# Gate and up products of ten feature tiles in the last two token blocks: seven half-width products in place of eight over four of five channel chunks, with sums of weights and tokens on VectorE

## The chip, the cores and the metric

The kernel runs on one core of a Trainium2 chip. The metric is the time of one execution on the device in microseconds (us), as the median of several runs. The core has five engines that run side by side and wait for each other by semaphores: PE (TensorE, matrix products into PSUM), DVE (VectorE), ACT (ScalarE), POOL (GpSimd) and SP (which only issues DMAs here). PEld is the loading of weights into PE.

## What is computed

A layer with linear attention and a gated two-layer network without a nonlinearity, on 2048 tokens of 640 channels in bf16:

```python
def _B_ref(x, w_gate, w_up, w_down):
    g = jnp.einsum("bsd,df->bsf", x, w_gate)
    u = jnp.einsum("bsd,df->bsf", x, w_up)
    h = g * u
    return jnp.einsum("bsf,fd->bsd", h, w_down)

x = A_x
h = x + _A_ref(_layernorm(x, axis=-1), A_wqkv, A_w_phi, A_wo)
h2 = h + _B_ref(_layernorm(h, axis=-1), B_w_gate, B_w_up, B_w_down)
return h2
```

`_A_ref` is the attention: query, key and value projections, softmax features of query and key with either sign, a product of key features with values, and its application to the query features. The change touches `g` and `u` of `_B_ref` alone. There are 640 channels (five chunks of 128) and 1536 features (twelve tiles of 128).

## The kernel before

The 2048 tokens are 16 tiles of 128 and four blocks of 512. Keys and values of all tiles come first, then block by block: queries (`q`, `Q`), the attention output (`n`, in `num`), its projection and the second layernorm (`h`, in `watt`), the gate and up products (`f`, in `fu`) and the down product (`d`, `D`). A transposed block of normalized tokens lies in `hT` (channels on the partitions, two buffers), the product of gate and up in `hhT` (features on the partitions, two buffers).

`fu(b, ft, j, n)` makes one feature tile of one block. PE runs two groups of five products (one per channel chunk), gate into the first bank of a PSUM buffer and up into the second. ScalarE copies the gate half to `gate`, and VectorE multiplies it with the up half in PSUM and writes `hhT`. Blocks 1 to 3 take 512 tokens at once, block 0 takes 256 twice.

The down product of most token tiles already uses a scheme of seven block products in place of eight (`down_pair`, with `weight_sums` on GpSimd and `block_sums` on VectorE, named `T` and `S` in the order). There, PE writes a product into a bank, a helper copies the intermediate value out (`snap`), and PE goes on adding to the same bank; VectorE adds copy and bank at the end (`fin`).

All operations are recorded with the data that they read and write, and then placed. What each engine does in which sequence is written out by hand in the table `ORDER`, one list of unit names per engine: `f3.2.0` is feature tile 2 of block 3, and each occurrence of a name stands for the next operation of that unit on that engine. `place` walks the lists, hands out buffers from pools in that sequence (four PSUM buffers of two banks, `p_ps`; two `gate` buffers) and `finish` turns the recorded dependences into semaphore waits. An engine works through its list strictly in sequence, so an instruction that waits holds all that stand behind it on that engine.

Lines: every group of products is issued by the helper `mms` (L620). The copy of the gate is L1093, the gate times up product L1095, the down scheme's copies L1190, its add on GpSimd L1192, its final sums L1197, its differences of `hhT` L1131. `ACT phik L896` are exponentials early in the kernel.

A profile names a tile by the storage it lies in. `BK` is called `phik`: it first holds the key features and later `hhT`, `hT` and the first half of `oT`. `phiqT` holds the transposed query features, `xT` the transposed input (and later the sums of `block_sums` and some of `weight_sums`), `Wp` the projection weights (and later sums of `weight_sums`), `vaug` the values and later the down weights.

Of the kernel before, what the change touches and what calls it, by code (L numbers as in the profile page):

```python
# [62 lines left out]

SNAP = {(3, 0): "AAAV", (3, 1): "AAAV"}
# [19 lines left out]
    "DVE":  # L84
# [323 lines left out]
def _build(ctx, nc, A_x, A_wqkv, A_w_phi, A_wo, B_w_gate, B_w_up, B_w_down, out):  # L408
# [74 lines left out]
    o1 = KH * HALF  # L483
    SH = [[xTf[:, o1 + KH * P * (2 * k + i):o1 + KH * P * (2 * k + i + 1)].rearrange("p (f n) -> p f n", f=KH) for i in range(2)]
          for k in range(4)]

    PS = [ctx.enter_context(nc.psum_tensor("ps%d" % i, [P, 2, 512], FP32)) for i in range(4)]

    p_ps, p_eq, p_ob, p_outb, p_t32, p_gate, p_junk = Pool(4), Pool(3), Pool(2), Pool(2), Pool(2), Pool(2), Pool(1)
# [849 lines left out]
```

## Time and profile before

| what | value |
|---|---|
| median of 3 runs | 274.58 us (273.94 to 274.63) |
| the profiled execution, its own time | 274.22 us |
| its span, first to last instruction | 272.2 us |
| instructions in the span | 5588 |
| PE busy | 266.9 us |
| DVE busy | 195.1 us |
| ACT busy | 139.7 us |
| POOL busy | 127.9 us |
| mean granted PE clock | 1.000 |

The time of a run is the span and what lies around it, 2.0 us in the profiled execution. A row of the timeline gives start, length, engine, line, operation, output and inputs by storage name, shapes, and in brackets how long the engine had been idle before and for whom it waited. A row of the groups gives the count, the busy time, the mean duration in ns, and the idle time before. The duration of a matmul includes its way through the array, in which the next one already runs: what it costs the engine is the distance between two starts.

### The profile page before, as it was taken

The page shows a single profiled execution, that of the slowest core. Times are in us where ns is not written, and L with a number is a line of the kernel's source. Part 1 is how long each engine was busy: PE and PEld are TensorE (multiplying, and loading weights), DVE is VectorE, ACT ScalarE, POOL GpSimd, SP SyncE. Part 2 cuts the span into 40 slices and gives each one's busy share as a digit, 9 for nine tenths or more (in the row PEclk, how much of TensorE's full clock was granted, in tenths as well). Part 3 has the DMA queues.
Part 4 walks back from the last instruction along what each step waited for, and adds up shares of the span by engine and source line. Part 5 has one row for each costly group of instructions (what it writes and reads, how often), then busy time and mean ns, then how long its engine had stood idle before and what let it go on. Part 6 is the DMA issues. An engine that isn't in the chain of part 4 may idle for free.

```text
span 272.2 us, 5588 instructions
## 1 busy us (share of the span) xinstructions
PE 266.9 (98%) x2216; PEld 181.7 (67%) x2229; DVE 195.1 (72%) x383; ACT 139.7 (51%) x261; POOL 127.9 (47%) x177
## 2 busy tenths in 40 slices
PE   8999999999999999999999999999999999999995
PEld 8877687777878887777865555555555464555673
DVE  1899999999999997887886685833754283522673
ACT  2568999999856767548165232164221230411411
POOL 5626989999842349064392833015340220130442
PEclk9999999999999999999999999999999999999999
DMA  7987899904175997445854454300043001001012
GB/s 192 291 148 182 139 281 400 333 2 88 25 106 101 162 287 105 97 80 102 113 116 80 79 104 72 72 2 0 0 96 99 0 0 51 0 6 42 4 69 75
DMA packets 67385, 28.60 MB, mean 105 GB/s; under 512 B 57632, under 2 KB 66080, under 8 KB 67360
## 3 DMA queue, kind: packets, MB, share of 16 engines
q1 hardware_dynamic: 66432, 27.90, 45.5%
q10 hardware_dynamic: 928, 0.35, 0.5%
q8 instruction: 17, 0.28, 0.5%
q14 instruction: 8, 0.07, 0.1%
HBM read 11.82 MB, written 2.62 MB: 53 GB/s over the span
## 4 chain that ended last, share of the span: by engine, by line
PE 78%; DVE 6%; ACT 4%; DMA 3%; POOL 3%; SPq 3%; issue 2%; ACTq 0%
PE ps L620 78%; SPq L516 3%; DMA Wp<-in_A_wqkv_dram 2%; DVE ps L888 1%; ACT phik L896 1%; DMA phiqT<-eq 1%; ACT eq L896 1%; DVE Wp L856 1%; DVE phik L1095 1%; POOL phik L913 1%; ACT vaug L919 1%; ACT junk L613 1%; DVE Sq L950 1%; DVE Ssum L910 1%; POOL eq L962 0%
## 5 line engine op out<-in xcount | busy, mean ns | idle before, releaser
L620 PE MATMUL ps<-phik,Wgu 128*128 128x512 bf16 (+1 forms) x587 | 108.4, 335 | 0.6
L620 PE MATMUL ps<-Wp,xT 128*128 128x320 bf16 (+1 forms) x606 | 88.9, 299 | 0.2 <-ACT phik L896 0.2
L620 PEld LDWEIGHTS ps<-phik,Wgu 128*128 128x128 bf16 x600 | 57.9, 98 | 41.7 <-DVE phik L1095 0.4
L620 PEld LDWEIGHTS ps<-Wp,xT 128*128 128x128 bf16 x606 | 58.3, 98 | 23.8 <-ACT phik L896 0.6
L1095 DVE TENSOR_TENSOR phik<-ps,gate 128x512 bf16<-128x512 f32 (+1 forms) x60 | 34.0, 575 | 40.8 <-PE ps L620 27.8
L1093 ACT ACTIVATE gate<-ps 128x512 bf16<-128x512 f32 (+1 forms) x60 | 29.8, 510 | 61.8 <-PE ps L620 53.6
L1192 POOL TENSOR_TENSOR eq<-eq,x_all 128x320 f32<-128x320 f32 x20 | 15.8, 797 | 65.8 <-ACT eq L1190 65.7
L913 POOL TENSOR_TENSOR phik<-phik,Rk 128x1280 bf16<-128x1280 bf16 x16 | 37.4, 2356 | 6.7 <-DVE Rk L912 6.5
L888 DVE TENSOR_REDUCE ps<-ps 128x1 f32<-128x640 f32 (+1 forms) x32 | 26.2, 821 | 0.9 <-PE ps L620 0.9
L620 PE MATMUL ps<-vaug,phik 128*128 128x63 bf16 (+1 forms) x308 | 26.0, 238 | 0.0
L950 DVE TENSOR_REDUCE Sq<-eq 128x66 f32<-128x1320 bf16 x16 | 24.2, 1509 | 2.5 <-ACT eq L896 2.5
L910 DVE TENSOR_REDUCE Ssum<-phik 128x64 f32<-128x1280 bf16 x16 | 23.5, 1469 | 0.4 <-ACT phik L896 0.2
L620 PEld LDWEIGHTS ps<-vaug,phik 128*128 128x128 bf16 x308 | 18.4, 97 | 6.2
L962 POOL TENSOR_TENSOR eq<-eq,rq 128x660 bf16<-128x660 bf16 x16 | 20.9, 1305 | 0.9
L896 ACT ACTIVATE eq<-ps,nb,rs 128x300 bf16<-128x300 f32 (+2 forms) x26 | 17.4, 692 | 7.1 <-DVE hb L1078 3.5
L1190 ACT ACTIVATE eq<-ps 128x320 f32<-128x320 f32 x20 | 8.5, 437 | 21.7 <-PE ps L620 21.7
L957 POOL TENSOR_TENSOR rq<-Sq,rq 128x33 f32<-128x33 f32 x16 | 4.1, 257 | 32.2 <-DVE rq L956 26.7
L896 ACT ACTIVATE eq<-ps,nb,nrs 128x300 bf16<-128x300 f32 (+2 forms) x26 | 17.4, 698 | 0.0
L613 ACT ACTIVATE junk<-x_all,nmh 128x640 bf16<-128x640 bf16 x14 | 11.6, 825 | 8.7 <-DVE x_all L1069 8.7
L896 ACT ACTIVATE phik<-ps,nb,rs 128x640 bf16<-128x640 f32 x16 | 14.3, 892 | 2.3 <-POOL rs L677 2.0
L896 ACT ACTIVATE phik<-ps,nb,nrs 128x640 bf16<-128x640 f32 x16 | 14.3, 897 | 0.0
L1197 DVE TENSOR_TENSOR outb<-ps,eq 128x320 bf16<-128x320 f32 x22 | 10.3, 485 | 5.6 <-PE ps L620 4.6
(107 smaller groups left out, 311.3 us busy)
## 6 DMA issues: line engine op xcount, KB each, us to landing
x_all<-in_A_x_dram SPq DMA_DIRECT2D x4, 640.0 KB, 10.6
out_dram<-outb SPq DMA_DIRECT2D x14, 160.0 KB, 1.8
Wgu<-in_B_w_gate_dram SPq DMA_DIRECT2D x1, 1920.0 KB, 10.7
Wgu<-in_B_w_up_dram SPq DMA_DIRECT2D x1, 1920.0 KB, 15.9
vaug<-in_B_w_down_dram SPq DMA_DIRECT2D x1, 1920.0 KB, 9.6
Wp<-in_A_wqkv_dram SPq DMA_DIRECT2D x1, 800.0 KB, 5.1
phiqT<-in_A_wqkv_dram SPq DMA_DIRECT2D x1, 800.0 KB, 6.7
Wo<-in_A_wo_dram SPq DMA_DIRECT2D x1, 800.0 KB, 6.4
```

The source lines that it names most:

```text
L613: g.op("ACT", lambda e: e.activation(out=junk[:, v.i, :], in_=in_, func=func, accum_out=acc, **more), rd=rd, wr=wr, use=[v], t=0.73, lat=0.97)
L620: ins = e.matmul(o_, lhsT=l_, rhs=r_, start=s_, stop=p_, skip_group_check=True)
L888: g.op("DVE", lambda e: e.tensor_reduce(out=mx(), in_=src(), axis=AX.XY if len(src().shape) == 3 else AX.X, op=ALU.max, apply_absolute_val ...
L896: g.op("ACT", lambda e, s=s, sc=sc, to=to, of=of: e.activation(out=to(s), in_=of(), func=ACT.Exp, bias=nb[:, i:i + 1], scale=sc[:, t:t + 1 ...
L910: g.op("DVE", lambda e: e.tensor_reduce(out=Ssum[:, vs.i, :], in_=x, axis=AX.X, op=ALU.add), rd=R_phik[t], wr=vs.R, use=[vs], t=1.39, lat=1.5)
L913: g.op("POOL", lambda e: e.tensor_tensor(out=x, in0=x, in1=Rk[:, vr.i, :].unsqueeze(2).to_broadcast([P, 2 * H, DH]), op=ALU.mult), rd=vr.R ...
L950: g.op("DVE", lambda e: e.tensor_reduce(out=Sq[:, vs.i, :].rearrange("p (w g) -> p w g", w=NQ), in_=feat(0, NQ).rearrange("p w (g f) -> p ...
L962: return e.tensor_tensor(out=x, in0=x, in1=rq[:, vr.i, :].rearrange("p (w h) -> p w h", h=HW).unsqueeze(3).to_broadcast([P, NQ, HW, DH]), ...
L1093: g.op("ACT", lambda e: e.activation(out=gate[:, vg.i, 0:P * n], in_=PS[v.i][:, 0, 0:P * n], func=ACT.Copy), rd=[v.R[0]], wr=vg.R, use=[v, ...
L1095: g.op("DVE", lambda e: e.tensor_tensor(out=hhT[:, hb, ft, sl], in0=PS[v.i][:, 1, 0:P * n], in1=gate[:, vg.i, 0:P * n], op=ALU.mult), rd=[ ...
L1192: g.op("POOL", lambda e: e.tensor_tensor(out=slot(x), in0=slot(x), in1=x_all[:, t, c], op=ALU.add), rd=x.R + [R_h[t]], wr=x.R, use=[x], t= ...
L1197: g.op("DVE", lambda e: e.tensor_tensor(out=outb[:, o_.i, HALF * half:HALF * (half + 1)], in0=PS[v.i][:, bk, 0:HALF], in1=slot(y), op=ALU. ...
```

## The change

For ten of the twelve feature tiles (0 to 9) of blocks 2 and 3, `fu` hands over to `fu_seven`. Take gate and up as two rows of weights, chunks 0, 1 and chunks 2, 3 as two columns, and the first and second 256 tokens of the block as two columns of tokens. The plain way has eight products of (two chunks) x (256 tokens); the new one has seven, with four sums of weights and four of tokens:

- weights, made once by `gate_sums` (`G`): G0 = up01 + up23, G1 = gate01 - up01, G2 = G0 - gate01, G3 = gate23 - G2, each for three groups of tiles (0 to 4, 5 to 7, 8 and 9), which lie in three storages that are no longer in use (`phiqT`, `xT`, `Wp`): twelve operations on VectorE;
- tokens, made once for each block by `token_sums` (`H`): H0 = t01' - t01, H1 = t23' - t01', H2 = t23' - H0, H3 = t23 - H2, where the prime means the second 256 tokens: four operations on VectorE.

The fifth chunk stays as it was, one product of 512 tokens for gate and one for up. So a tile has 14 products of 256 columns and 2 of 512, in place of 10 of 512. PE's work on a tile is six operations: gate01 x t01 into the up bank, G0 x H0 into the gate bank, G2 x H2 added to the up bank, gate23 x t23 and G3 x t23' and the fifth chunk in the gate bank, G1 x H1 added to the up bank, up23 x H3 and the fifth chunk in the up bank. Between them ScalarE copies four intermediate halves (256 columns of fp32) to `halves`, in the storage of the second `phiqT` buffer; there are five such copy buffers of 512 columns. PE may add to a bank only after the copy is out. At the end VectorE adds copy and bank for gate (L1196) and for up (L1198), and multiplies the two, bf16 from SBUF (L1200).

The diff, with the table of the order cut to a line:

```diff
+SEVEN = {2: range(10), 3: range(10)}
+WSP = ()
...
-        "f2.11.0 D1.0 f2.6.0 D1.1 f2.7.0 D1.1 f2.6.0 f2.7.0 f3.2.0 f3.2.0 f2.5.0 f2.5.0 D1.1 D1.1 D1.1 D1.1 f3.9.0 D1.1 f3.6.0 "
+        "f2.5.0 f3.2.0 f3.2.0 f3.9.0 f3.9.0 D1.1 f3.9.0 f3.2.0 f3.9.0 f3.2.0 f3.2.0 f3.9.0 f3.6.0 f3.6.0 f3.2.0 f3.0.0 f3.0.0 "
...
+    GW = [(0, 5, [pq[:, 1280 * k:1280 * (k + 1)] for k in range(4)]), (5, 3, [xTf[:, o1 + 768 * k:o1 + 768 * (k + 1)] for k in range(4)]),
+          (8, 2, [Wp[:, k, 0:512] for k in range(4)])]
+    HS = [oTa[:, k, :].rearrange("p (c n) -> p c n", c=2) for k in range(4)]
+    halves = pq[:, NQ * 512:NQ * 512 + 5 * 1024].bitcast(FP32).rearrange("p (i n) -> p i n", i=5)
...
+    p_hb, p_slot, p_half = Pool(2), Pool(8), Pool(5)
...
+        if ft in SEVEN.get(b, ()):
+            return fu_seven(b, ft)
...
+    def gate_sums():
+        for k, (x, y, op) in enumerate((((1, 0), (1, 2), ALU.add), ((0, 0), (1, 0), ALU.subtract), (0, (0, 0), ALU.subtract),
+                                        ((0, 2), 2, ALU.subtract))):
+            for r, (f0, nf, _) in enumerate(GW):
+                U("G%d.%d" % (r, k))
...
+                g.op(eng, lambda e, part=part, x=x, y=y, op=op, r=r, k=k: e.tensor_tensor(out=gw(r, k), in0=part(x), in1=part(y), op=op),
+                     rd=rd, wr=[R_GW[r][k]], t=t, lat=t + 0.12, port=True)
+
+    def token_sums(b):
...
+            g.op("DVE", lambda e, part=part, x=x, y=y, op=op, k=k: e.tensor_tensor(out=HS[k], in0=part(x), in1=part(y), op=op),
+                 rd=rd, wr=[R_HS[k]], t=0.34, lat=0.46, port=True)
+
+    def fu_seven(b, ft):
...
+        v, vg = Buf(p_ps, 2), Buf(p_gate)
+        s = [Buf(p_half, 2) for _ in range(2)]
...
+        def snap(bk, i, h):
+            g.op("ACT", lambda e: e.activation(out=halves[:, s[i].i, 256 * h:256 * (h + 1)], in_=PS[v.i][:, bk, 256:512], func=ACT.Copy),
+                 rd=[v.R[bk]], wr=[s[i].R[h]], use=[v, s[i]], after=HALF_USERS, t=0.3, lat=0.42)
+
+        U("f%d.%d.0" % (b, ft))
+        mm([(raw(0, 0), tok(0, 0), 256, 256)], 1, True)
+        snap(1, 0, 0)
+        mm([(summed(0), toks(0), 256, 256)], 0, True)
+        snap(0, 1, 1)
+        mm([(summed(2), toks(2), 256, 256)], 1)
+        snap(1, 0, 1)
+        mm([(raw(0, 2), tok(2, 0), 0, 256), (summed(3), tok(2, 1), 256, 256), (raw(0, 4), tok(4, 0, 2), 0, 512)], 0)
+        mm([(summed(1), toks(1), 256, 256)], 1)
+        snap(1, 1, 0)
+        mm([(raw(1, 2), toks(3), 0, 256), (raw(1, 4), tok(4, 0, 2), 0, 512)], 1)
+        R_out = R_hhT[hb_][ft]
+        g.op("DVE", lambda e: e.tensor_tensor(out=gate[:, vg.i, :], in0=PS[v.i][:, 0, :], in1=halves[:, s[0].i, :], op=ALU.add),
+             rd=[v.R[0]] + s[0].R, wr=vg.R, use=[v, s[0], vg], t=0.61, lat=0.73)
+        g.op("DVE", lambda e: e.tensor_tensor(out=hhT[:, hb_, ft, :], in0=PS[v.i][:, 1, :], in1=halves[:, s[1].i, :], op=ALU.add),
+             rd=[v.R[1]] + s[1].R, wr=R_out, use=[v, s[1]], t=0.61, lat=0.73)
+        g.op("DVE", lambda e: e.tensor_tensor(out=hhT[:, hb_, ft, :], in0=hhT[:, hb_, ft, :], in1=gate[:, vg.i, :], op=ALU.mult),
+             rd=R_out + vg.R, wr=R_out, use=[vg], t=0.34, lat=0.46, port=True)
...
     weight_sums()
...
+    gate_sums()
     ffn(0)
...
+    token_sums(2)
     ffn(2)
...
+    token_sums(3)
     ffn(3)
```

The table of the order is new for all engines. Two places in block 3 show what it does around the new tiles. The first is on PE, where tiles 0 and 6 of block 3 are made. Before, with `ps` and its number the PSUM buffer, `phik` the tokens and `Wgu` the weights of gate or up, and tile 6 in ps2, tile 0 in ps1, tile 9 in ps3:

```order
L620 MATMUL ps2<-phik,Wgu 128x512 [waits s_DVE]
L620 MATMUL ps2<-phik,Wgu 128x512 x4
L620 MATMUL ps1<-phik,Wgu 128x512 [waits s_DVE]
L620 MATMUL ps1<-phik,Wgu 128x512 x4
L620 MATMUL ps2<-phik,Wgu 128x512 x5
L620 MATMUL ps3<-phik,Wgu 128x512 x5
```

The same place now; `phiqT`, `xT` and `Wp` hold the sums of weights, and tile 0 is in ps2, tile 3 in ps3, tile 6 in ps0:

```order
L1174 MATMUL ps2<-phik,Wgu 128x256 [waits s_ACT]
L1174 MATMUL ps2<-phik,Wgu 128x256
L1174 MATMUL ps2<-phik,phiqT 128x256 x2
L1174 MATMUL ps2<-phik,Wgu 128x512
L1174 MATMUL ps0<-phik,xT 128x256 [waits s_ACT]
L1174 MATMUL ps0<-phik,xT 128x256
L1174 MATMUL ps2<-phik,phiqT 128x256 x2
L1174 MATMUL ps3<-phik,Wgu 128x256 x2
L1174 MATMUL ps3<-phik,phiqT 128x256 x2
L1174 MATMUL ps0<-phik,Wgu 128x256 [waits s_ACT]
L1174 MATMUL ps0<-phik,Wgu 128x256
L1174 MATMUL ps0<-phik,Wgu 128x512
```

Where PE ran five products of one tile in a row and waited for VectorE to free a buffer, it now goes back and forth between three tiles, and waits for ScalarE's copies in the middle of a tile. Between the product in ps0 that is copied (the two with `xT`) and the next one that waits in ps0 stand six products of 256 columns.

The second place is on VectorE, with the tiles of the middle of block 3. Before, each tile has one row (L1095), with a difference for the down product (L1131) and final sums (L1197) between them:

```order
L1095 TENSOR_TENSOR phik<-ps0,gate 128x512 [waits s_ACT,s_PE]
L1095 TENSOR_TENSOR phik<-ps2,gate 128x512 [waits s_ACT]
L1095 TENSOR_TENSOR phik<-ps3,gate 128x512 [waits s_PE]
L1131 TENSOR_TENSOR xT<-phik,xT 128x768
L1095 TENSOR_TENSOR phik<-ps1,gate 128x512 [waits s_ACT]
L1197 TENSOR_TENSOR outb<-ps0,eq 128x320 [waits d_out2,s_POOL,s_PE]
```

Now each tile has three rows, the gate sum (L1196), the up sum (L1198) and their product (L1200); the `phiqT` in a sum is the copy buffer:

```order
L1198 TENSOR_TENSOR phik<-ps1,phiqT 128x512 [waits s_PE]
L1198 TENSOR_TENSOR phik<-ps0,phiqT 128x512 [waits s_PE]
L1200 TENSOR_TENSOR phik<-phik,gate 128x512 [waits s_DVE]
L1196 TENSOR_TENSOR gate<-ps2,phiqT 128x512 [waits s_DVE]
L1200 TENSOR_TENSOR phik<-phik,gate 128x512
L1198 TENSOR_TENSOR phik<-ps2,phiqT 128x512 [waits s_PE]
L1196 TENSOR_TENSOR gate<-ps3,phiqT 128x512 [waits s_DVE,s_ACT,s_PE]
L1198 TENSOR_TENSOR phik<-ps3,phiqT 128x512 [waits s_PE]
L1200 TENSOR_TENSOR phik<-phik,gate 128x512 [waits s_DVE]
L1196 TENSOR_TENSOR gate<-ps1,phiqT 128x512 [waits s_DVE,s_ACT,s_PE]
```

The rows of several tiles are interleaved, and the product of a tile stands one or more rows behind its up sum. An up sum is what frees a PSUM buffer and its copy buffers for the next tile.

More of the change, by code (lines that the diff above doesn't have):

```diff
@@ L1096, in fu, with gw, part @@
              rd=[v.R[1]] + vg.R, wr=R_hhT[hb][ft][j:j + n], use=[v, vg], t=0.073 + 0.134 * n, lat=0.19 + 0.134 * n)
+    def gw(r, k):
+        return GW[r][2][k].rearrange("p (c n) -> p c n", c=2)
+    def gate_sums():
[3 more added lines that the diff above has]
+                U("G%d.%d" % (r, k))
+                def part(q, r=r, f0=f0, nf=nf):
+                    return gw(r, q) if isinstance(q, int) else Wgu[:, q[0], q[1]:q[1] + 2, P * f0:P * (f0 + nf)]
+                rd = R_Wgu + [R_GW[r][q] for q in (x, y) if isinstance(q, int)]
+                eng, t = ("POOL", 0.1 + 0.47 * nf) if r in WSP else ("DVE", 0.06 + 0.14 * nf)
+                g.op(eng, lambda e, part=part, x=x, y=y, op=op, r=r, k=k: e.tensor_tensor(out=gw(r, k), in0=part(x), in1=part(y), op=op),
+                     rd=rd, wr=[R_GW[r][k]], t=t, lat=t + 0.12, port=True)
@@ new lines, in token_sums, with part @@
+    def token_sums(b):
+        hb_ = b % 2
+        for k, (x, y, op) in enumerate((((0, 1), (0, 0), ALU.subtract), ((2, 1), (0, 1), ALU.subtract), ((2, 1), 0, ALU.subtract),
+                                        ((2, 0), 2, ALU.subtract))):
+            U("H%d.%d" % (b, k))
+            def part(q):
+                return HS[q] if isinstance(q, int) else hT[:, hb_, q[0]:q[0] + 2, 256 * q[1]:256 * (q[1] + 1)]
+            rd = [R_HS[q] for q in (x, y) if isinstance(q, int)] + [R_hT[hb_][2 * q[1] + i] for q in (x, y) if not isinstance(q, int)
+                                                                    for i in range(2)]
+            g.op("DVE", lambda e, part=part, x=x, y=y, op=op, k=k: e.tensor_tensor(out=HS[k], in0=part(x), in1=part(y), op=op),
+                 rd=rd, wr=[R_HS[k]], t=0.34, lat=0.46, port=True)
@@ new lines, in fu_seven, with raw, summed, tok @@
+    def fu_seven(b, ft):
+        hb_ = b % 2
+        v, vg = Buf(p_ps, 2), Buf(p_gate)
+        s = [Buf(p_half, 2) for _ in range(2)]
+        r = max(r for r in range(len(GW)) if GW[r][0] <= ft)
+        f0 = P * (ft - GW[r][0])
+        def raw(gu, c0):
+            return lambda c: Wgu[:, gu, c0 + c, P * ft:P * (ft + 1)], R_Wgu[gu]
+        def summed(k):
+            return lambda c: gw(r, k)[:, c, f0:f0 + P], R_GW[r][k]
+        def tok(c0, i, n=1):
+            return lambda c: hT[:, hb_, c0 + c, 256 * i:256 * (i + n)], R_hT[hb_][2 * i:2 * (i + n)]
+        def toks(k):
+            return lambda c: HS[k][:, c, :], [R_HS[k]]
+        def mm(lst, bk, first=False):
+            def f(e):
+                ins, fr = None, first
+                for l_, r_, lo, n in lst:
+                    for c in range(2 if n == 256 else 1):
+                        ins = e.matmul(PS[v.i][:, bk, lo:lo + n], lhsT=l_[0](c), rhs=r_[0](c), start=fr, stop=False, skip_group_check=True)
+                        fr = False
+                return ins
+            t = sum(0.2185 if n == 256 else 0.216 for _, _, _, n in lst)
+            g.op("PE", f, rd=[x for l_, r_, _, _ in lst for x in [l_[1]] + r_[1]], wr=[v.R[bk]], use=[v], t=t, lat=t + 0.15)
+        def snap(bk, i, h):
[19 more added lines that the diff above has]
+             rd=R_out + vg.R, wr=R_out, use=[vg], t=0.34, lat=0.46, port=True)
@@ L1297, in _build @@
     g.alias([r for x in R_S for r in x], R_xT[2:12])
+    g.alias(R_GW[0], [r for x in R_phiqT[0] for r in x])
+    g.alias(R_GW[1], R_xT[11:])
+    g.alias(R_GW[2], R_Wp[0])
+    gate_sums()
     ffn(0)
@@ L1302, in _build @@
     down(0)
+    g.alias(R_HS, R_oT[0])
+    HALF_USERS += [o for x in R_phiqT[1] for r in x for o in r.w + r.r]
+    token_sums(2)
     ffn(2)
```

5 lines of the change are left out of this document (3 added, 2 removed), and 99 rows, old and new, of the table ORDER.

## The prediction

> **What bounds the kernel now.** I read the page first (busy shares, slices, the chain that ended last), then TensorE's waits, then the busy times by stage, then single stretches of the timeline. The page:
>
> ```profile
> PE 266.9 (98%) x2216; PEld 181.7 (67%) x2229; DVE 195.1 (72%) x383; ACT 139.7 (51%) x261; POOL 127.9 (47%) x177
> ...
> DVE  1899999999999997887886685833754283522673
> ...
> PEclk9999999999999999999999999999999999999999
> ...
> PE 78%; DVE 6%; ACT 4%; DMA 3%; POOL 3%; SPq 3%; issue 2%; ACTq 0%
> ```
>
> PE is busy for 98% of the 272.2 us span, at the full granted clock in every slice, and 78% of the chain is PE. VectorE is full only up to about the middle and has gaps behind it. All that PE ever waited for, by the list of waits:
>
> ```profile
> PE ps L620 <- PEq L1324: 0.8, 1, 0.8
> PE ps L620 <- DVE Phi L1003: 0.3, 1, 0.3
> PE ps L620 <- ACT phik L896: 0.2, 1, 0.2
> ```
>
> That is 1.3 us in three waits, none of them in a gate/up product. So the time is the length of PE's queue, and a shorter queue ends sooner unless PE begins to wait. The stages that the change touches (columns: length; busy us and instructions of PE, PEld, DVE, ACT, POOL; clock; DMA share; GB/s):
>
> ```profile
> 139.00:157.00 18.00, 17.89 (x129) 9.95 (x129) 12.54 (x23) 7.46 (x14) 11.86 (x15) 1.00 0.41 84
> 157.00:175.00 18.00, 17.84 (x113) 9.62 (x114) 12.20 (x26) 5.68 (x11) 3.94 (x7) 1.00 0.49 92
> 175.00:198.00 23.00, 22.89 (x135) 13.19 (x135) 12.66 (x24) 9.54 (x21) 7.43 (x13) 1.00 0.00 1
> 198.00:227.00 29.00, 28.79 (x156) 15.55 (x159) 13.16 (x26) 7.13 (x14) 5.44 (x8) 1.00 0.22 57
> 227.00:256.00 29.00, 28.89 (x160) 15.75 (x161) 11.36 (x20) 7.78 (x16) 5.53 (x7) 1.00 0.04 13
> ```
>
> Nearly all gate/up tiles of blocks 2 and 3 lie in the last two rows: PE 57.7 of 58 us, VectorE 24.5, ScalarE 14.9. There is idle time on both helpers to spend there; the question is whether it lies where the new work falls.
>
> **The change, part by part.** *Products removed.* What a matmul costs PE is the distance to the next start, not its own duration. Ten 512-column products (one tile) and ten 256-column ones (a tile of block 0), each with the row behind it:
>
> ```profile
> 132.73 1.25 PE L620 MATMUL ps<-phik,Wgu 128*128 128x256 bf16 x10
> 133.82 1.53 PE L620 MATMUL ps<-Wp,xT 128*128 128x300 bf16 x10
> ...
> 199.25 2.32 PE L620 MATMUL ps<-phik,Wgu 128*128 128x512 bf16 x10
> 201.41 0.98 PE L620 MATMUL ps<-Wp,xT 128*128 128x320 bf16 x6
> ...
> L620 PEld LDWEIGHTS ps<-phik,Wgu 128*128 128x128 bf16 x600 | 57.9, 98 | 41.7 <-DVE phik L1095 0.4 <-issue 0.3
> ```
>
> 201.41 - 199.25 = 2.16 us, 0.216 each; 133.82 - 132.73 = 1.09 us, 0.109 each, with one weight load of 98 ns per product hidden in it. A tile goes from 10 x 0.216 = 2.16 us to 14 x 0.109 + 2 x 0.216 = 1.958 us: 0.202 us saved, 20 x 0.202 = 4.04 us in all. The Trainium skill ("TensorE: Matmul & The Clock Gate", section "Back-to-back issue gap") speaks against it: a stream of load and matmul pairs is said to run at about 81 ns for 128 columns and 131 ns for 512. A straight line gives about 98 ns at 256 (an estimate from that page), a tile would go from 1.31 to 1.63 us, and the change would cost PE 6.4 us. The trace does not agree: 0.216 and 0.109 us in this very loop.
>
> *Copies added on ScalarE, sums on VectorE.* Their nearest rows, by shape, then pairs that ran back to back:
>
> ```profile
> L1095 DVE TENSOR_TENSOR phik<-ps,gate 128x512 bf16<-128x512 f32 x36 | 24.4, 686 | 36.7 <-PE ps L620 23.7 <-ACT gate L1093 13.0
> L1093 ACT ACTIVATE gate<-ps 128x512 bf16<-128x512 f32 x36 | 20.9, 594 | 43.4 <-PE ps L620 35.3 <-DVE phik L1095 8.1
> L1093 ACT ACTIVATE gate<-ps 128x256 bf16<-128x256 f32 x24 | 9.0, 385 | 18.4 <-PE ps L620 18.3
> L1131 DVE TENSOR_TENSOR xT<-phik 128x768 bf16<-128x768 bf16 x14 | 7.8, 569 | 5.8 <-PE ps L620 5.7
> ...
> 133.48 0.66 ACT L1093 ACTIVATE gate<-ps 128x256 bf16<-128x256 f32 x2 [2.96 <-PE ps L620]
> 194.85 1.08 ACT L1093 ACTIVATE gate<-ps 128x512 bf16<-128x512 f32 x2 [1.72 <-PE ps L620]
> ...
> 134.66 0.74 DVE L1095 TENSOR_TENSOR phik<-ps,gate 128x256 bf16<-128x256 f32 x2
> 207.56 1.29 DVE L1095 TENSOR_TENSOR phik<-ps,gate 128x512 bf16<-128x512 f32 x2 [2.20 <-PE ps L620]
> 230.88 1.02 DVE L1131 TENSOR_TENSOR xT<-phik 128x768 bf16<-128x768 bf16 x2
> ```
>
> Subtracting one duration from a pair gives what an instruction costs its queue. ScalarE: 256 columns 0.66 - 0.385 = 0.275, 512 columns 1.08 - 0.594 = 0.49. A tile goes from 0.49 to 4 x 0.275 = 1.10 us; 20 tiles add 12.2 us, to some 27 of about 54 us in the last two stages: room enough. VectorE: a sum from PSUM 1.29 - 0.686 = 0.605 (256 columns: 0.33, so about 0.06 fixed); a bf16 sum of 768 from SBUF 1.02 - 0.55 = 0.47. No 512 one is shown: between 512/768 of it, 0.31, and 0.47; with the fixed 0.06 it is 0.335, which I take. A tile goes from 0.605 to 2 x 0.605 + 0.335 = 1.545 us; 20 tiles add 18.8 us. The eight token sums (512 long) are 8 x 0.335 = 2.7 us. The twelve weight sums (1280, 768, 512 long) are 4 x (0.74 + 0.47 + 0.335) = 6.2 us by the same line; if 1280 ran at the per-element cost of the PSUM rows it would be 4 x 1.4 for that group, 2.6 us more. Most of them fall between 139 and 198 us, where VectorE is busy 37.4 of 59 us; about 45 with them. I cost them at nothing: PE's tiles of blocks 0 and 1 hide them. Were that cover gone, a late weight sum would hold PE by its own length, 0.3 to 0.8 us. The last two stages rise to 24.5 + 18.8 + about 3 = 46 of 54 us.
>
> *The new waits of PE.* Four times per tile PE may add to a bank, or use it again, only after ScalarE has copied it; everything behind it in PE's queue waits along. The paired down products do this already:
>
> ```profile
> 235.46 0.98 PE L620 MATMUL ps<-vaug,phik 128*128 128x320 bf16 x6
> 236.28 1.79 PE L620 MATMUL ps<-Wp,xT 128*128 128x320 bf16 x12
> 236.48 0.44 ACT L1190 ACTIVATE eq<-ps 128x320 f32<-128x320 f32 x1 [1.21 <-PE ps L620]
> 237.29 0.44 ACT L1190 ACTIVATE eq<-ps 128x320 f32<-128x320 f32 x1 [0.38 <-PE ps L620]
> ...
> 31.97 0.91 ACT L896 ACTIVATE phik<-ps,nb,nrs 128x640 bf16<-128x640 f32 x1
> ...
> 32.93 0.85 PE L620 MATMUL ps<-Wp,xT 128*128 128x320 bf16 x5 [0.22 <-ACT phik L896]
> ```
>
> The copy starts 236.48 - 236.28 = 0.20 us after its group's last product has given way; a 256 copy takes 0.385; and PE starts about 0.05 us after ScalarE ends (32.93 - 32.88). A round trip is 0.635 us. In the new order I count the PE work between a copied product and the one that waits for it (0.218 us per pair, 0.652 and 0.434 for the groups with the fifth chunk, 0.815 per down group): of 80 such distances the shortest is 0.654 (three places, one in the piece shown above), the next 0.81. So PE just fits. Each of the three may still expose part of a 98 ns weight load: 0 to 0.3 us, I take 0.2.
>
> *VectorE in block 3.* The tightest stretch, counted in the order from the gate sum of tile 9 to the up sum of tile 5: PE has 29 x 0.218 + 8 x 0.652 + 8 x 0.434 = 15.0 us there, VectorE 15 sums, 8 products and 5 differences before the last sum: 15 x 0.605 + 8 x 0.335 + 5 x 0.47 = 14.1 us. That is 94%: VectorE fits if it never waits, and PE waits for it for a free bank pair or copy buffer if it falls behind by more than these hold. The lower bound of the loss is 0; the upper one takes full durations instead of queue costs (15 x 0.686 + 8 x 0.42 + 5 x 0.569 = 16.5 us; 0.42 is 0.335 plus the 0.08 that a row's duration exceeds its cost by): 1.5 us. I take 0.4, near the lower end, since neighbours in VectorE's new order mostly belong to different tiles. GpSimd's adds can stretch an SBUF difference; that is small and rare:
>
> ```profile
> 221.60 0.79 POOL L1192 TENSOR_TENSOR eq<-eq,x_all 128x320 f32<-128x320 f32 x1 [0.84 <-ACT eq L1190]
> ...
> 222.14 0.66 DVE L1131 TENSOR_TENSOR xT<-phik 128x768 bf16<-128x768 bf16 x1
> 222.84 0.56 DVE L1131 TENSOR_TENSOR xT<-xT,phik 128x768 bf16<-128x768 bf16 x1
> ```
>
> *The re-dealt order.* Elsewhere the same products come in another sequence, with SP's and POOL's steps among them. PE had 1.3 us of waits to win or lose: 0, with 0.3 us to either side.
>
> *Sum.* -4.04 + 0.2 + 0.4 = -3.4 us. The profiled execution took 274.22 us, span 272.2 and 2.0 around it, and would take 270.8. It lies 0.4 us under the median of the runs, 274.58; on that the sum gives 271.2 us.
>
> **The rivals.** *VectorE becomes the limit.* For it: 94% in block 3, and PE holding at most four bank pairs. Against it: plain and down tiles before and behind let VectorE catch up. Price: 1.5 us in block 3 instead of 0.4, up to as much again in block 2; 274.58 - 4.04 + 1.5 = 272.0 to 273.5 us.
>
> *Waits expose weight loads: slower.* In the new order 57 groups of these tiles carry a wait for ScalarE. If a load can't be fetched past such a wait, each shows its 98 ns: 57 x 0.098 = 5.6 us, so 276.1 us. It decides from 4.04 / 0.098 = 41 exposed loads on. Against it: the third of the down groups in the rows above waits for ScalarE, yet the two groups from 236.28 on run through without a gap; there the copy was back 0.18 us early, here 0.02 to 0.2 at the tight places.
>
> *The sums come late.* If weight and token sums push back what VectorE does for block 2's attention output between 139 and 198 us, PE stands until its tokens are there. It takes some 3.4 us of such waits to be at 274.6; with 21 us of idle VectorE in those rows this needs bad placement: 274.0 to 274.9 us.
>
> *The clock drops.* Many short groups with small gaps could lower the granted clock; each us at half clock loses 0.5 us, so 8 us of that take all the gain, 275 us or more. The rows show 1.00 in every stage, also where PE waited. The Trainium skill (the same page, section "A second HAM failure mode: psum-queue depth-cycling") describes such swings; by that rule this kernel is a candidate, but the trace shows no sign so far.
>
> That the products are not really fewer can be left out: the order shows fourteen 256-column and two 512-column products per tile.
>
> **How the numbers follow.** Forecast (270.2 to 272.0) 0.60; VectorE the limit (272.0 to 273.5) 0.24; late sums 0.08; exposed loads 0.06; clock 0.02. The low end is all of 4.04 with 0.3 from the new order: 270.2. The range 270.2 to 273.5 holds 0.84. A measurement of this kernel can tell about 0.3%, 0.8 us, from no change: faster by more than that 0.84, within it 0.08, slower 0.08.
>
> **What would show it.** Right: 160 fewer 512-column and 280 more 256-column gate/up products, these 0.109 us apart; PE busy near 263 us; 80 copies of about 0.385 us; VectorE near 228 us busy (195.1 + 20 x 1.11 for the tiles + some 10 for the sums, by durations); PE's waits under 2 us. VectorE as the limit shows as PE waiting for VectorE in block 3; exposed loads as some 0.1 us before most groups that wait for ScalarE; late sums as a hole before the first tiles of block 2. The prediction is wrong if copies or sums take over 0.1 us more than these rows, or if the 256-column products, now with sums as weights, are further apart.

## The result and the profile after

The changed kernel takes 271.25 us (median of 4 runs, 271.03 to 271.54), the kernel before 274.55 us beside it (273.94 to 274.63). The ratio is 0.9885, with a 95% interval from 0.9868 to 0.9902. Forecast were 271.2 us and faster. The profiled execution took 271.18 us with a span of 269.1: 3.1 us less span than before.

The page of the changed kernel, in the lines that were shown of before:

```profile
PE 264.0 (98%) x2349; PEld 192.5 (72%) x2349; DVE 222.8 (83%) x443; ACT 154.7 (57%) x321; POOL 129.0 (48%) x177
...
DVE  1999999999999897789888669898876678977763
...
PEclk9999999999999999999999999999999999999999
...
PE 83%; DVE 5%; DMA 4%; ACT 3%; POOL 2%; issue 2%; SPq 1%; ACTq 0%; DVEq 0%
```

PE is still the bound (98%, and 83% of the chain), VectorE's valley in the second half of the slices is filled, and the clock stays at full speed. The list of waits has three rows of PE:

```profile
PE ps L641 <- PEq L1437: 0.8, 1, 0.8
PE ps L641 <- DMA vaug<-ob: 0.7, 1, 0.7
PE ps L641 <- DVE Phi L1024: 0.3, 1, 0.3
```

The first and the last stood in the list of before. The wait for a DMA is new, and it is not at a gate/up product. The two stages of the new tiles, and 15 us in the middle of block 3 (columns as in the prediction):

```profile
198.00:227.00 29.00, 29.00 (x222) 21.12 (x220) 20.82 (x43) 15.07 (x45) 7.82 (x12) 1.00 0.13 36
...
223.00:238.00 15.00, 15.00 (x122) 11.40 (x120) 14.14 (x28) 9.27 (x29) 0.21 (x1) 1.00 0.01 2
```

VectorE works 14.14 of 15.00 us there, and PE works all 15. (A product of 256 columns counts as busy for 273 ns and gives way after 109, so a stop of up to 0.16 us does not show in PE's column, and a longer one is 0.16 us longer than a row's brackets say.) The groups of the new work by shape:

```profile
L1181 ACT ACTIVATE phiqT<-ps 128x256 f32<-128x256 f32 x80 | 26.8, 385 | 26.6 <-PE ps L1174 24.0 <-DVE phik L1198 1.3 <-DVE gate L1196 1.1
L1174 PE MATMUL ps<-phik,Wgu 128*128 128x256 bf16 x120 | 22.6, 273 | 0.0
L1196 DVE TENSOR_TENSOR gate<-ps,phiqT 128x512 bf16<-128x512 f32 x20 | 13.7, 686 | 1.1 <-PE ps L1174 0.3 <-ACT phiqT L1181 0.3
L1198 DVE TENSOR_TENSOR phik<-ps,phiqT 128x512 bf16<-128x512 f32 x20 | 13.7, 686 | 3.7 <-PE ps L1174 3.6
L1200 DVE TENSOR_TENSOR phik<-phik,gate 128x512 bf16<-128x512 bf16 x20 | 8.4, 425 | 0.1
...
L1134 DVE TENSOR_TENSOR phiqT<-Wgu 128x1280 bf16<-128x1280 bf16 x2 | 1.6, 790 | 0.0
```

The durations are those taken from before: copies 385 ns, sums 686 ns, the 512 bf16 product, which had no row, at 425 ns where 420 was set, and a weight sum of 1280 near 0.8 us, far from the upper bound of 1.4. By the groups the new work is 32.4 us on VectorE (35.8 for the tiles and 10.3 for the sums, less 13.7 for the 20 products gone), as forecast; its busy time rose by only 27.7 us, to 222.8 and not 228, because the page counts time in which two neighbours overlap only once (all groups of VectorE add up to 216.7 us before and 249.1 after, 32.4 more). PE's 264.0 us stand against the 263 forecast.

**Where the 3.1 us come from.** Four places of PE's timeline before, and the issue of a DMA that matters below:

```profile
82.97 0.72 PE L527 MATMUL ps<-ident,x_all 128*128 128x128 bf16 x10
...
100.91 2.52 SPq L516 DMA_TRANSPOSE vaug<-ob  x1
...
104.13 1.80 PE L620 MATMUL ps<-phik,Wgu 128*128 128x256 bf16 x15
105.77 1.53 PE L620 MATMUL ps<-Wo,vaug 128*128 128x320 bf16 x10
...
109.38 1.25 PE L620 MATMUL ps<-phik,Wgu 128*128 128x256 bf16 x10
110.77 1.40 PE L620 MATMUL ps<-Wo,vaug 128*128 128x320 bf16 x9
...
268.26 0.98 PE L620 MATMUL ps<-vaug,xT 128*128 128x320 bf16 x6
```

And after; the row of a DMA, from the chain, stands in a fence of its own:

```profile
83.15 0.72 PE L548 MATMUL ps<-ident,x_all 128*128 128x128 bf16 x10
...
104.18 0.71 PE L641 MATMUL ps<-phik,Wgu 128*128 128x256 bf16 x5
105.59 1.54 PE L641 MATMUL ps<-Wo,vaug 128*128 128x320 bf16 x10 [0.70 <-DMA vaug<-ob]
...
265.19 0.98 PE L641 MATMUL ps<-vaug,xT 128*128 128x320 bf16 x6
```

```profile
100.93 4.61 DMA vaug<-ob
```

The first and the last of these rows are the same work in both kernels. The last starts 268.26 - 265.19 = 3.07 us earlier, the first 0.18 us later, so 3.25 us are gained between them. Near 105 us PE takes the projection of token tile 5 (L641 with `Wo`, unit `h5`), which needs its attention output transposed by a DMA. The changed kernel issues that DMA at 100.93 us, and it lands at 105.54. Before, PE reached the place only at 105.77, and did not wait: it had three groups of block 0 ahead of it (15 products of 0.109 us, from 104.13 on). After, only one group (5 products, 0.55 us) stands there, and PE stops from 104.73 to 105.59: 0.86 us. But the place on PE is only half of it. Before, the same DMA was issued at the same time, 100.91 us, and landed 3.6 us later, near 104.5; after, it took 4.61 us. Had it landed as before, PE at 104.73 would not have waited.

Before had stops of its own nearby: 0.30 us (109.38 + 10 x 0.109 = 110.47, and the next at 110.77) and 0.16 us just before 104.13. The list of waits shows neither: a stop counts there only beyond its first 0.16 us, and what is left of these is too short. Both are gone after. Inside the new tiles I find 0.13 us of stops in all, one of 0.10 us near 218.8 us and the rest near 225. So -4.04 + 0.86 - 0.30 - 0.16 + 0.13 = -3.51, against -3.25 measured. Of the 0.26 us between, 0.12 are two small stops of the changed kernel near 136 and 163 us; the rest I did not find.

The forecast of -3.4 us is met, but not by its own terms. The 0.6 us set for the new tiles shrank to 0.13. What lies outside them was set at 0 and cost 4.04 - 3.25 - 0.13 = 0.66 us between the two rows. The 0.18 us by which the first row is late need not be the order's: in the eleven profiled kernels whose lists are the same up to there, this row starts anywhere from 83.03 to 83.57 us.

### The profile page after: what moved, and what is told of

The parts are those of the page before. It is cut to its first block, busy times and chain, and to the rows that moved or that the text cites. A ratio compares the mean times of both kernels' runs of the same rounds, so it can differ in the third digit from the quotient of the medians.

```text
span 269.1 us, 5986 instructions
## 1 busy us (share of the span) xinstructions
PE 264.0 (98%) x2349; PEld 192.5 (72%) x2349; DVE 222.8 (83%) x443; ACT 154.7 (57%) x321; POOL 129.0 (48%) x177
## 4 chain that ended last, share of the span: by engine, by line
PE 83%; DVE 5%; DMA 4%; ACT 3%; POOL 2%; issue 2%; SPq 1%; ACTq 0%; DVEq 0%
PE ps L641 68%; PE ps L1174 15%; DMA Wp<-in_A_wqkv_dram 2%; DMA vaug<-ob 2%; DVE Wp L877 1%; ACT phik L917 1%; DVE ps L909 1%; SPq L537 1%; POOL phik L934 1%; ACT vaug L940 1%; ACT junk L634 1%; DVE phik L1118 0%; PE ps L548 0%; POOL rs L698 0%; DVE Ssum L931 0%
## 5 line engine op out<-in xcount | busy, mean ns | idle before, releaser
L641 PE MATMUL ps<-Wp,xT 128*128 128x320 bf16 (+1 forms) x606 | 89.1, 299 | 0.1
L641 PEld LDWEIGHTS ps<-Wp,xT 128*128 128x128 bf16 x606 | 58.2, 98 | 22.9 <-ACT phik L917 0.5
L641 PE MATMUL ps<-phik,Wgu 128*128 128x256 bf16 (+1 forms) x400 | 65.7, 315 | 0.0
L1297 POOL TENSOR_TENSOR eq<-eq,x_all 128x320 f32<-128x320 f32 x21 | 17.2, 819 | 73.8 <-ACT eq L1295 73.5
L641 PEld LDWEIGHTS ps<-phik,Wgu 128*128 128x128 bf16 x400 | 38.2, 98 | 20.0 <-DVE phik L1118 0.6
L1181 ACT ACTIVATE phiqT<-ps 128x256 f32<-128x256 f32 x80 | 26.8, 385 | 26.6 <-PE ps L1174 24.0
L1116 ACT ACTIVATE gate<-ps 128x256 bf16<-128x256 f32 (+1 forms) x40 | 18.4, 468 | 32.2 <-PE ps L641 31.6
L1174 PE MATMUL ps<-phik,Wgu 128*128 128x256 bf16 (+1 forms) x160 | 32.4, 299 | 0.0
L1118 DVE TENSOR_TENSOR phik<-ps,gate 128x256 bf16<-128x256 f32 (+1 forms) x40 | 20.5, 523 | 8.2 <-PE ps L641 6.6
L641 PE MATMUL ps<-vaug,phik 128*128 128x63 bf16 (+1 forms) x308 | 26.0, 238 | 0.0
L641 PEld LDWEIGHTS ps<-vaug,phik 128*128 128x128 bf16 x308 | 18.3, 97 | 5.0
L1174 PEld LDWEIGHTS ps<-phik,Wgu 128*128 128x128 bf16 x160 | 15.1, 98 | 5.6 <-ACT phiqT L1181 0.2
L1295 ACT ACTIVATE eq<-ps 128x320 f32<-128x320 f32 x21 | 9.2, 438 | 14.5 <-PE ps L641 14.5
```

What stands on the lines that cost most here:

```text
L641: ins = e.matmul(o_, lhsT=l_, rhs=r_, start=s_, stop=p_, skip_group_check=True)
L1116: g.op("ACT", lambda e: e.activation(out=gate[:, vg.i, 0:P * n], in_=PS[v.i][:, 0, 0:P * n], func=ACT.Copy), rd=[v.R[0]], wr=vg.R, use=[v, ...
L1118: g.op("DVE", lambda e: e.tensor_tensor(out=hhT[:, hb, ft, sl], in0=PS[v.i][:, 1, 0:P * n], in1=gate[:, vg.i, 0:P * n], op=ALU.mult), rd=[ ...
L1174: ins = e.matmul(PS[v.i][:, bk, lo:lo + n], lhsT=l_[0](c), rhs=r_[0](c), start=fr, stop=False, skip_group_check=True)
L1181: g.op("ACT", lambda e: e.activation(out=halves[:, s[i].i, 256 * h:256 * (h + 1)], in_=PS[v.i][:, bk, 256:512], func=ACT.Copy), rd=[v.R[bk ...
L1297: g.op("POOL", lambda e: e.tensor_tensor(out=slot(x), in0=slot(x), in1=x_all[:, t, c], op=ALU.add), rd=x.R + [R_h[t]], wr=x.R, use=[x], t= ...
```

## The experiments

Theory A: the products save 4.04 us, what the new tiles add is hidden (copies by distance, VectorE by a margin of 6%, sums in their gaps), and 0.7 us go to the order far from the tiles. Rivals: the saving is another, VectorE or the round trips already take part of it, or the sums do. The experiments ran on three chips; each ratio is to the kernel before on the same chip (274.05 to 274.42 us).

**Plain tiles in the new order.** All 20 tiles made by ten products of 512 at the places of the new ones, without sums of weights and tokens:

```diff
-SEVEN = {2: range(10), 3: range(10)}
+SEVEN = {}
...
-    gate_sums()
```

> All tiles of blocks 2 and 3 are made the plain way again (ten products of 512, one copy, one product on VectorE, no weight or token sums), but every engine keeps the new order, with the plain operations at the places of the fourth and sixth group of a seven-product tile, the fourth copy and the last VectorE row. My theory: the new tiles themselves save all of 4.04 us less 0.1, and the new order costs 0.8 us elsewhere, most of it one hole of 0.86 us in PE's queue at 104.7 us. Then this kernel is slower than the kernel before, by 0.6 to 0.9 us: 275.2 us, with the hole at 105 us still there. The rival, that the new order is neutral and the tiles save only 3.3 us of their 4.04 because of waits in blocks 2 and 3: 274.5 us, no slower than before.

Measured: 279.14 us, 1.0181 [1.0163, 1.0198]; span 277.5. Theory and rival (275.2 and 274.5 us) both missed. A row of PE's timeline:

```profile
204.21 1.25 PE L633 MATMUL ps<-phik,Wgu 128*128 128x512 bf16 x5 [1.11 <-DVE outb L1294]
```

PE stops for 1.11 + 0.16 = 1.27 us here, and three times more (1.34 at 206, 1.27 at 246, 0.75 at 251 us), each time for an operation of VectorE. Probably a plain tile needs its buffers at once, where the new order hands them out for tiles in pieces. The order does not suit plain tiles, so this kernel does not isolate it. It does give the saving: 269.1 + 4.04 + 4.63 of stops, less the 0.13 of the new tiles and 0.09 that the stop near 105 us is shorter, is 277.55, and 277.5 was measured.

**One block alone.** The same edit for block 2 (so that only block 3 has new tiles), and for block 3:

```diff
-SEVEN = {2: range(10), 3: range(10)}
+SEVEN = {3: range(10)}
```

> Seven products in block 3 only; the tiles of block 2 are plain at the places of the new order, without token sums for block 2. Half of the saved PE work is undone: 10 x 0.202 = 2.02 us. My theory (no stalls in the new tiles): 271.25 + 2.0 = 273.25 us. If VectorE at 94% in block 3 cost time there (up to 1.5 us), block 2 would be worth more than block 3: 273.5 to 274.0 us here.

> Seven products in block 2 only; block 3 plain at the places of the new order, without token sums for block 3. My theory: 273.25 us, the same as with block 3 alone. If VectorE cost time in block 3, undoing block 3 loses less than 2.0 us: 272.0 to 272.9 us.

Measured: block 3 alone 275.90 us, 1.0063 [1.0048, 1.0078], span 273.9; block 2 alone 274.90 us, 1.0020 [1.0009, 1.0032], span 273.1. Both missed by stops of the same kind in the plain block (1.27 and 1.34 us near 203 and 206, and 0.50 at 223; 1.27 and 0.74 near 242 and 247). With ten tiles' saving given back, 269.1 + 2.02, plus these stops and less what is shorter elsewhere, the spans come to 273.9 and 273.1. Each block is worth half of 4.04 us, to about 0.1 us.

**The late transpose, PE's side.** `h5` two groups of block 0 later in PE's list, where it stood before:

```diff
-n4 f0.3.2 h5 f0.7.2 f0.3.2 f0.7.2
+n4 f0.3.2 f0.7.2 f0.3.2 h5 f0.7.2
```

> The changed kernel with one unit moved on PE alone: the attention projection of token tile 5 (h5) stands behind two more gate/up groups of block 0, where the kernel before has it. My theory: the hole of 0.86 us before h5 is a transfer that lands at about 105.5 us whatever PE does, and 1.09 us of products fit in front of it: 270.4 to 270.6 us and no wait of PE for the transposed tile. The rival: what stands behind is just as tight, the wait turns up at the next unit: 271.2 us.

Measured: 271.41 us, 0.9895 [0.9878, 0.9911]. No gain; the rival was right. PE's timeline:

```profile
106.34 1.54 PE L646 MATMUL ps<-Wo,vaug 128*128 128x320 bf16 x10
...
108.94 1.54 PE L646 MATMUL ps<-Wp,xT 128*128 128x300 bf16 x10 [0.50 <-DVE x_all L1095]
```

`h5` now starts without a wait, at 106.34 instead of 105.59 (0.4 us of that is an execution that is late from its start on). VectorE's add of its result (`x_all`) frees the buffer that the queries at 108.94 need, and a stop (0.50 + 0.16 = 0.66 us) appears there instead.

**The late transpose, the queue's side.** The DMA of token tile 5 ahead of those of tiles 2 and 3 in SyncE's list, and `h5` ahead of one group of block 0 in PE's:

```diff
-h2 h3 n5
+n5 h2 h3
...
-n4 f0.3.2 h5 f0.7.2
+n4 h5 f0.3.2 f0.7.2
```

> The changed kernel with one transposing DMA moved: the attention output of token tile 5 is transposed ahead of the normalized tokens of tiles 2 and 3 instead of behind them in SyncE's queue, and PE takes the projection that uses it ahead of one group of block 0 instead of behind it. In the changed kernel the DMA was issued at 100.93 us, landed near 105.5 and PE stood for 0.86 us for it. Theory: that hole is the order's doing and goes, nothing else is late, 270.4 us and a hole under 0.2 us there. Rival: SyncE's queue is full from 95 to 110 us, so the hole only changes its owner (block 0's tokens, or the next transpose, land later by the same 1.3 us): 271.0 to 271.6 us.

Measured: 270.57 us (270.29 to 272.20), 0.9870 [0.9839, 0.9901]; span 268.6. The stop is gone:

```profile
103.99 0.49 PE L646 MATMUL ps<-Phi,phiqT 128*128 128x63 bf16 x11
104.33 1.53 PE L646 MATMUL ps<-Wo,vaug 128*128 128x320 bf16 x10
```

PE runs through; one stop of 0.14 us stays near 110 us. The DMA is now issued at 98.01 us and lands 3.7 us later, 2.6 us ahead of PE. It is its earlier place in the queue that removes the stop, since the other move only makes PE ask for it sooner. The theory was right: two moves in the table take most of the 0.86 us back, and the span is 0.5 us shorter than the changed kernel's. The intervals of the two ratios overlap, so that this version beats the changed kernel rests on the traces, not yet on the times.

**The old order up to block 1.** The lists of before up to the unit where each holds the same work in both kernels (PE's `n8`, VectorE's `h6`, and so on), the new ones behind that:

> The changed kernel, but every engine follows the list of the kernel before up to about 115 us (to n8 on PE, h6 on VectorE, the second step of q14 on ScalarE, T2 on GpSimd, Q10 on the DMA queue) and the new list behind it; the same units stand on either side of these cuts. My theory: the hole of PE at 104.7 us (0.86 us) comes from the new sequence of that stretch as a whole, not from one unit, so the old sequence closes it and 270.4 to 270.7 us remain. The rival: the hole is a matter of when transposed tiles land and moves on as it did when h5 alone was moved: 271.2 us.

Measured: 282.72 us, 1.0304 [1.0281, 1.0327]; span 280.9. Two things show. The first is near 105 us (the window of this answer ends at 105 us, so its row counts 3 of the 15 products):

```profile
104.70 0.49 PE L646 MATMUL ps<-phik,Wgu 128*128 128x256 bf16 x3 [0.56 <-issue]
...
106.47 1.54 PE L646 MATMUL ps<-Wo,vaug 128*128 128x320 bf16 x10
```

All engines follow the lists of before here, and up to 103.64 us PE's rows start when they did before. Yet PE then stops for 0.74 us ahead of 104.70 and for 0.13 us ahead of `h5`, 0.87 us together, and `h5` starts 0.70 us later than before. The profile names no engine for the first stop; by issue and landing, it ends as the transposed tokens of tile 3 land (about 104.6 us, where before they landed at about 104.1). The DMA of `h5` was issued at 101.91 us here and landed at 105.5, as late as in the changed kernel. So the old lists do not bring back the early landing of before, and the theory is not borne out. Why the transpose landed about 1 us earlier in the profile of before stays open.

The second is a far larger stop at the seam. GpSimd's timeline, SyncE's and PE's around it:

```profile
152.91 0.25 POOL L983 TENSOR_TENSOR rq<-Sq,rq 128x33 f32<-128x33 f32 x1 [8.03 <-DVE rq L982]
...
156.54 2.52 SPq L542 DMA_TRANSPOSE phiqT<-eq  x2
159.10 2.92 SPq L542 DMA_TRANSPOSE phik<-ob  x2
161.78 2.85 PE L646 MATMUL ps<-Wo,phik 128*128 128x320 bf16 x10 [7.64 <-DMA phik<-ob]
```

VectorE's reciprocal for the query features (`rq`) stands behind weight sums and other work in its list and ends at 152.8 us; GpSimd had stood idle for 8.03 us for it; SyncE holds the transposes of `ob` behind those of GpSimd's `eq`; and PE waits 7.64 us. The ends of five lists that were cut at the same work don't fit each other in time. The time of this kernel is therefore no measure of the order; as a warning, each list is only good with the other four.

**Shorter distances.** The last group of several new tiles moved forward on PE, so that 0.218 or 0.436 us of other products stand between the copied product and it, where the change has 0.654 or more; for instance:

```diff
-f2.4.0 f2.0.0 f2.10.0 f2.2.0 f2.0.0 f2.4.0
+f2.4.0 f2.0.0 f2.4.0 f2.2.0 f2.10.0 f2.0.0
```

> The changed kernel with the last group of eleven seven-product tiles moved forward on PE, so that in eight tiles only one or two pairs of 256-column products (0.218 or 0.436 us) stand between the product that is copied last and the group that waits for the copy. If a round trip is 0.635 us and nothing else is lost, PE waits 5 x 0.417 + 3 x 0.2 = 2.7 us more: 273.9 us. If each such wait also shows a weight load of 98 ns, 0.8 us more: 274.7 us. If copies come back in a quarter microsecond, there is nothing to wait for: 271.3 us.

Measured: 276.13 us, 1.0069 [1.0051, 1.0087], 4.9 us more than the changed kernel by the medians; the profiled execution was the slowest of six (277.17 us, span 275.1). Two places of the timeline, PE and ScalarE:

```profile
217.19 0.60 PE L1179 MATMUL ps<-phik,xT 128*128 128x256 bf16 x4
217.60 0.66 ACT L1186 ACTIVATE phiqT<-ps 128x256 f32<-128x256 f32 x2 [0.53 <-PE ps L1179]
218.04 1.04 PE L1179 MATMUL ps<-phik,Wgu 128*128 128x256 bf16 x6 [0.26 <-ACT phiqT L1186]
...
225.03 1.09 ACT L1186 ACTIVATE phiqT<-ps 128x256 f32<-128x256 f32 x3 [1.08 <-PE ps L1179]
225.05 0.38 PE L1179 MATMUL ps<-phik,Wgu 128*128 128x256 bf16 x2
226.18 1.04 PE L1179 MATMUL ps<-phik,Wgu 128*128 128x256 bf16 x6 [0.75 <-ACT phiqT L1186]
```

At the first, the copied pair has given way at 217.41, its copy runs from 217.60, and PE goes on at 218.04: 0.63 us, the 0.635 of the prediction, of which 0.218 is covered. At the second the copy is the third in ScalarE's row, and PE stops for 0.91 us. That is one reason why the loss is larger than expected: a round trip is 0.635 us only when ScalarE is free; each copy ahead adds up to 0.275. Five stops that name ScalarE make 3.5 us together, and two that name VectorE another 0.9.

**VectorE one product longer.** One more 512 bf16 product per new tile on VectorE, whose result isn't used:

```diff
+        g.op("DVE", lambda e: e.tensor_tensor(out=gate[:, vg.i, :], in0=gate[:, vg.i, :], in1=hhT[:, hb_, ft, :], op=ALU.mult), ...
```

> The changed kernel with one more bf16 product of 512 on VectorE right behind the last one of each seven-product tile, into the gate buffer that nobody reads any more: 0.335 us and about 0.08 us of waiting for its neighbour, 20 times. In the tight stretch of block 3 VectorE then needs 14.1 + 8 x 0.42 = 17.4 us against 15.0 of PE. My theory (VectorE is just under the limit, buffers hold some 0.6 us): PE begins to wait for VectorE, 1.8 us in block 3 and about 0.5 us in block 2: 273.5 us. If VectorE has more reserve than these counts say: 271.3 us.

Measured: 274.37 us, 1.0004 [0.9987, 1.0021]; span 272.4, so 3.3 us for 20 x 0.335 = 6.7 us of work, where 2.3 were expected. The windows by stage:

```profile
198.00:224.00 26.00, 26.00 (x199) 18.93 (x197) 21.05 (x44) 13.10 (x38) 7.90 (x12) 1.00 0.14 40
...
224.00:239.00 15.00, 13.84 (x102) 8.88 (x100) 14.44 (x30) 8.40 (x25) 0.00 (x0) 1.00 0.00 1
```

Block 2's tiles hide their half almost wholly (0.19 us of stops up to 224 us). From there on VectorE is at 96% and PE at 92%: stops of 0.14 to 0.72 us, some 3.0 us in all. The ten products of block 3 are 3.35 us, and the change had left nearly no room for them.

**Sums twice.** Every sum of weights and of tokens issued twice in a row; then only those of weights, then only those of tokens:

```diff
-                g.op(eng, lambda e, part=part, ...: e.tensor_tensor(out=gw(r, k), in0=part(x), in1=part(y), op=op),
+                for _ in range(2):
+                    g.op(eng, lambda e, part=part, ...: e.tensor_tensor(out=gw(r, k), in0=part(x), in1=part(y), op=op),
```

> The changed kernel with every weight sum and every token sum made twice, the second time right behind the first and into the same place: 20 more VectorE operations, 9 us. My theory: the sums lie beside PE's tiles and cost nothing, so twice the sums cost little: 271.3 to 271.6 us. If the sums hold something up already, a doubled price shows: 272 us or more.

> The changed kernel with each of the twelve sums of weights issued twice in a row, the token sums once: about 6.2 us more VectorE, most of it between 147 and 185 us. With weight and token sums doubled together the span grew by 5.5 us, with holes of 0.93 to 1.86 us between 168 and 182 us and of 0.8 us near 229 us. Theory: the weight sums, twelve long instructions strewn among the normalizations of block 2 and 3, own the holes between 150 and 182 us, so 274.5 to 275.5 us here, and no hole near 229 us. Rival: the token sums, which stand directly ahead of the first new tiles of a block, own them all; then this kernel is within 0.5 us of the changed one, 271.2 to 271.8 us.

> The changed kernel with each of the eight sums of tokens issued twice in a row, the weight sums once: about 2.7 us more VectorE, half ahead of block 2's new tiles near 170 to 182 us, half ahead of block 3's near 200 to 225 us. Theory: only the holes near 178 and 229 us appear, 0.5 to 1.0 us in all, so 271.8 to 272.3 us. Rival: the token sums own all the holes of the doubled sums, 274 to 276 us. With cover for both halves it would stay at 271.2 us.

Measured: both 276.33 us, 1.0075 [1.0060, 1.0090], span 274.6 (5.5 us more than the changed kernel); weights alone 274.25 us, 0.9992 [0.9973, 1.0011], span 272.2 (3.1 more); tokens alone 272.46 us, 0.9921 [0.9892, 0.9950], span 270.4 (1.3 more). For the first I expected next to nothing, and was wrong: the cover is thin. The split came out as the theory of the second and third had it, though weights cost a little less and tokens a little more than their ranges. With the weight sums doubled, VectorE and PE near 170 us:

```profile
168.89 1.68 DVE L1141 TENSOR_TENSOR phiqT<-Wgu 128x1280 bf16<-128x1280 bf16 x2
...
170.76 0.81 DVE L1096 TENSOR_TENSOR x_all<-ps,x_all 128x640 bf16<-128x640 f32 x1
...
171.73 0.38 PE L1181 MATMUL ps<-phik,Wgu 128*128 128x256 bf16 x2 [0.73 <-DVE x_all L1096]
```

The sum of 1280 stands between a normalization and the add that frees PE's buffer; twice as long, it delays the add, and PE stops for 0.73 + 0.16 = 0.89 us. With the token sums doubled, PE stops for 0.46 us near 178 us, and for 0.29 and 0.39 us near 225 us, just ahead of block 3's tight stretch.

## Why the prediction was right, point by point

*Products removed, -4.04 us.* Right. A product of 256 columns keeps its 0.109 us with sums as weights as well, and the spans with plain tiles in one block, the other or both agree with 0.202 us per tile to about 0.1 us in all. PE from after's timeline, in the piece with the shortest distance:

```profile
225.81 0.38 PE L1174 MATMUL ps<-phik,xT 128*128 128x256 bf16 x2
226.03 0.38 PE L1174 MATMUL ps<-phik,phiqT 128*128 128x256 bf16 x2
226.22 1.21 ACT L1181 ACTIVATE phiqT<-ps 128x256 f32<-128x256 f32 x4 [0.58 <-PE ps L1174]
226.24 0.38 PE L1174 MATMUL ps<-phik,Wgu 128*128 128x256 bf16 x2
226.46 0.38 PE L1174 MATMUL ps<-phik,phiqT 128*128 128x256 bf16 x2
226.68 0.82 PE L1174 MATMUL ps<-phik,Wgu 128*128 128x256 bf16 x5
```

Each pair starts 0.22 us behind the one before. By the estimate from the 81 and 131 ns of the Trainium skill ("TensorE: Matmul & The Clock Gate", section "Back-to-back issue gap") the kernel would have become 6.4 us slower; it became 3.3 us faster, so they don't hold here.

*Copy round trips, +0.2.* Their size was right, 0.635 us, as the shorter distances show. In the rows above, the pair at 225.81 gives way at 226.03, its copy ends near 226.61, and PE uses the bank again at 226.68 without a stop: 0.654 us is enough, by 0.02 us. So the term was too large: no part of the exposed weight loads came true, and that rival is out.

*VectorE in block 3, +0.4.* The load was right: 14.14 of 15.00 us, 94%. The loss was 0.13 us at most, so this term was too large as well. VectorE can lag without stopping PE as long as copy buffers and banks hold out; one product more per tile, and it stops PE for 3.0 us. The rival "VectorE the limit" lay less than one such product per tile away. And a late VectorE reaches PE by a way round: in the row of the copies above, ScalarE was idle for 2.4 us for VectorE's sums (1.3 and 1.1), whose copy buffers it needs. In the kernel with one product more on VectorE, PE then waits for ScalarE (three of its stops name it).

*Weight and token sums, 0.* Right for this kernel: no stop of PE stands behind a sum. But the reason given, 21 us of idle VectorE in those stages, was no measure of the slack. Of 6.2 us more weight sums 3.1 came through to the end, of 2.7 us more token sums 1.1 to 1.3. The size set for a lost cover, 0.3 to 0.8 us for one sum, fits the 0.89 us measured only roughly.

*The re-dealt order, 0 with 0.3 to either side.* This step failed. Outside the new tiles 0.66 us were lost, and 0.86 at one DMA alone. The reason given was that PE had 1.3 us of waits to win or lose; a wait that is not there yet does not stand in that list, nor do the stops of 0.30 and 0.16 us that PE had near 104 and 110 us. How much of the 0.66 us is the order's stays open. `h5` stands 1.09 us further forward on PE, which is the order's doing. But its transposed tile also landed 1.0 us later than before, and that happened with the old lists as well. What could have been seen blind is a thin margin, not the stop: with the landing of before (104.5 us), PE would have come 0.2 us behind it.

*The clock.* 1.00 in every stage, as predicted. What it takes to lower it, the last section shows.

The mechanism was right: 4.04 us of products, nearly all of it kept. That the total of 271.2 us was met so closely is luck: 0.5 us too much for the tiles and 0.7 us too little for all else nearly cancel.

## What to carry to other kernels

Where an order is written anew, list the DMAs that land just barely before PE needs them, with the landing time from the trace of before, and count for each the PE work that now stands ahead of it; a wait that was covered is not in any list of waits. Leave them a margin: here the same transpose took 3.6 to 4.8 us to land in kernels that issued it at nearly the same time. The busy share of a helper in a stage does not tell its slack: look at whose buffer each added instruction delays, and test the slack by doubling the instruction. For products that go through a copy, the distance in PE work between the copied product and the next use of its bank must exceed one round trip plus the copies queued ahead of it, and then the copy is free.

## What the runs showed of the hardware

The stop of 7.64 us in the kernel with the old head lowered PE's clock. Its windows (the column ahead of the DMA share is the granted clock):

```profile
157.00:160.00 3.00, 0.00 (x0) 0.00 (x0) 0.00 (x0) 0.00 (x0) 2.92 (x3) 0.81 0.55 109
160.00:161.70 1.70, 0.00 (x0) 0.00 (x0) 0.00 (x0) 0.00 (x0) 0.68 (x1) 0.50 0.50 101
...
164.00:165.00 1.00, 1.00 (x6) 0.63 (x5) 0.33 (x2) 0.00 (x0) 0.00 (x0) 0.50 0.62 123
165.00:166.00 1.00, 1.00 (x6) 0.55 (x5) 0.57 (x1) 0.40 (x1) 0.00 (x0) 0.66 0.53 103
166.00:167.00 1.00, 1.00 (x7) 0.55 (x6) 0.11 (x1) 0.79 (x3) 0.31 (x2) 1.00 0.98 193
```

The clock is 0.50 from 160 to 165 us. So 0.81 over the 3 us ahead of it is half speed for the last 1.1 us of them, and the clock fell some 4.7 us after PE had stopped (161.78 - 7.64 = 154.14 us). The 0.66 from 165 to 166 us puts its rise at about 165.7, some 4 us after PE had resumed. Nearly 4 us at half speed cost about 2 us on top of the stop (an estimate from these rows). Stops up to 1.86 us, in the kernel with all sums doubled, left it at full speed. The Trainium skill ("TensorE: Matmul & The Clock Gate", section "HAM oscillation — how this bites in real kernels") gives idle gaps of over about 3.4 us as what lowers the clock; these runs agree, with nothing between 1.86 and 7.64 us to place the limit.
